# Two PSUM tiles of one bank in place of one tile of two banks, under a transformer block's dense products

## The chip, the cores and the metric

The kernel runs on one core of a Trainium2 chip. The metric is the device time of one execution in microseconds, as a median over runs. The engines are named as in the profile: PE is TensorE's matmuls and PEld its weight loads, DVE is VectorE, ACT is ScalarE, POOL is GpSimd, SP is SyncE, which issues most DMAs here.

## The reference

```python
xn = _layernorm(x)                      # x: 2048 x 512
qkv = xn @ wqkv                         # 32 heads of 16
scores = einsum("bhqd,bhkd->bhqk", q, k) * 16 ** -0.5
o = einsum("bhqk,bhkd->bhqd", softmax(scores), v)
A = o.reshape(B, S, D) @ wo
z = gelu(einsum("bsd,df->bsf", xn, w_in))          # 2048 x 1792
g = einsum("ts,bsf->btf", w_sp, _layernorm(z[..., 896:])) + b_sp
Bm = einsum("bsf,fd->bsd", z[..., :896] * g, w_out)
return x + A + Bm
```

So attention with 32 small heads and a gated MLP with a spatial product run side by side on the same normalised rows, all in float32.

## The kernel before

The kernel keeps attention going as a steady stream on PE and fills the room between with the dense products of everything else. Attention has three operations on PE: maxima (L1259; query by key, whose rowwise maximum DVE takes in L840), scores (L1245; key by query, whose exponential ACT takes in the helper of L86), and values (L1352; four column tiles of 32, eight key tiles in one stretch of 32 matmuls). These three rotate through three PSUM tiles `sl`, each of two banks.

The dense products use a fourth PSUM tile, `dps`, of two banks as well. A dense product runs as pairs of matmuls on 64 rows each: the upper half of the array writes bank 0 while the lower half writes bank 1, then a second pass swaps the halves (`both`, `dense`, L1310). When such a unit is complete, its generator yields the readers:

- `qk_out`, `v_out`, `z2_out` and `z1_out` (12, 5, 16 and 14 units on `dps`): ACT copies bank 0 out, DVE copies bank 1 out.
- `sp_out` and `sp_lone` (the spatial product): DVE multiplies both banks, in two operations.
- `out_` in `mlp_out` (8 units) and `out_` in `attn_out` (8 units): DVE adds the whole tile of 1024 columns to a tile in SBUF, in one operation.

The order of the instructions on each engine is fixed while the program is built, by a planner written in Python. It keeps a clock for each engine (`T`), gives each step a cost (`yield "D", td(512)` is 0.68 us of DVE), takes, when an engine comes free, the task of lowest priority number that is ready, and holds dense matmuls back until `dfree`, the time when it thinks that the readers are done (`rel`). Work that yields twice gives way to whatever was ready in between:

```python
ends[0] = T[k[0]] = s0 + k[1]
queue_up(k[5], k[3], k[4], ends[0] + 0.08)
```

The semaphores are not written by hand: the framework derives them from which tile an instruction reads or writes. On the chip each engine then runs its instructions strictly in the planned order.

Before the planner's stage there is an opening (class `First`, `STEPS`), whose order is written out by hand. It takes its accumulators in turn from `(dps, *sl)`: every fourth one is `dps`. Among these are 4 of the 16 first maxima (L1137 on `dps`). The opening's `n` normalises the two halves of one `xs` tile on two engines, one half on POOL (L1055) and one on ACT (L86). While dense products have no data, a `filler` (L1324) multiplies zeros into the same two banks, to keep PE running.

Of the kernel before, what the change touches and what calls it, by code (L numbers as in the profile page):

```python
# [8 lines left out]
F32 = mybir.dt.float32  # L9
F32R = mybir.dt.float32r  # L10
AF = mybir.ActivationFunctionType
ALU = mybir.AluOpType
AX = mybir.AxisListType
# [3 lines left out]
P = 128  # L17
S = 2048
D = 512
H = 32  # L20
DH = 16
# [47 lines left out]
def fused_block(ctx, tc, x, wqkv, wo, w_in, w_spT, b_sp, w_out, out):  # L69
    nc = tc.nc  # L70
# [5 lines left out]
    ps = ctx.enter_context(tc.tile_pool(name="ps", bufs=1, space=PSUM))  # L76
# [8 lines left out]
    def act(out, in_, func, **kw):  # L85
        return nc.scalar.activation(out, in_, func, **kw)  # L86

    def ta(n):
        return 0.2 + n / 1220.0

    def td(n):
        return 0.15 + n / 960.0
# [6 lines left out]
    zeror = cp.tile([P, P], F32R, name="zeror")  # L99
# [3 lines left out]
    brow = cp.tile([P, 512], F32R, name="brow")  # L103
# [26 lines left out]
    cscr = dr.tile([1, S], F32, name="cscr")  # L130
    bscr = [dr.tile([P, D], F32, name=f"bscr{t}") for t in range(NT)]

    dps = ps.tile([P, 2, 512], F32, tag="d", name="dps", bufs=1)
    sl = [ps.tile([P, 2, 512], F32, tag=f"s{i}", name=f"sl{i}", bufs=1) for i in range(3)]

    steady = []
# [4 lines left out]
    def move(dst, src):  # L141
        nc.sync.dma_start(raw(dst), raw(src))  # L142
# [36 lines left out]
    def lease(tag, n):  # L179
        room[tag] += n  # L180
# [11 lines left out]
    def spawn(gen, prio=2, ready=None):  # L192
        count[0] += 1
        ends[0] = clock() if ready is None else ready
        queue_up(gen, prio, count[0], ends[0])
# [40 lines left out]
    def t512(nm):  # L236
        return big.tile([P, 512], F32, tag="t512", name=nm, bufs=4)
# [125 lines left out]
    def rel():  # L363
        held[0] -= 1
        if not held[0]:
            dfree[0] = ends[0] + 0.1
# [12 lines left out]
    def qk_out(m, g, a):  # L379
        raw_ = t512(f"qr{m}_{a}_{g}")  # L380
        if a == 0:
            yield "A", ta(512)
            act(raw_, dps[:, 0, :], AF.Copy)
        else:
            yield "D", td(512)
            nc.vector.tensor_copy(raw_, dps[:, 1, :])
        rel()
        spawn(qk_split(m, g, a, raw_), 2, ends[0] + 0.08)

# [30 lines left out]
    vdone = {}  # L420

    def v_out(t, bank, k):
        src = (dps if k is None else sl[k])[:, bank, :].rearrange("p (h d) -> p h d", d=DH)
        if bank:
            yield "D", td(512)
            nc.vector.tensor_copy(vhead[:, t, :, :DH], src)
        else:
            yield "A", ta(512)
            act(vhead[:, t, :, :DH], src, AF.Copy)
        if k is None:  # L430
            rel()
        else:
            free_slot(k)
        vdone[t] = ends[0] + 0.1
# [30 lines left out]
    def z2_out(t, z, j):  # L465
        if j == 0:
            yield "A", ta(448)
            act(z[:, 0:448], dps[:, 0, :448], AF.Copy)
        else:
            yield "D", td(448)  # L470
            nc.vector.tensor_copy(z[:, 448:896], dps[:, 1, :448])
        rel()
        if not held[0]:
            spawn(z2_norm(t, z), 2, ends[0] + 0.08)
# [90 lines left out]
    def z1_out(f, g, bank):  # L565
        if bank == 0:
            yield "C", lambda: room["t5"] > 1
            lease("t5", -2)
            x, u = t512(f"z1x_{g}_{f}"), t512(f"z1u_{g}_{f}")
        else:  # L570
            z = piece(f"z1_{g}_{f}")
            x, u = z.bitcast(F32)[:, 0, :], z.bitcast(F32)[:, 1, :]
        if bank == 0:
            yield "A", ta(512)
            act(x, dps[:, 0, :], AF.Copy)
        else:
            yield "D", td(512)
            nc.vector.tensor_copy(x, dps[:, 1, :])
        rel()
        spawn(z1_gelu(f, g, bank, x, u), 2, ends[0] + 0.08)  # L580

# [136 lines left out]

    def sp_out(g, f, bank, z1):
        yield "D", 0.68  # L720
        nc.vector.scalar_tensor_tensor(z1, dps[:, bank, :], 0.5, z1, ALU.mult, ALU.mult)
        rel()
        spawn(h_split(g, f, z1), 2, ends[0] + 0.08)

    def sp_lone(g, f, z1):
        z1b = t512(f"z1b{g}")
        yield "D", 0.68
        nc.vector.scalar_tensor_tensor(z1b, dps[:, 0, :], 0.5, z1, ALU.mult, ALU.mult)
        yield "D", 0.68
        nc.vector.scalar_tensor_tensor(z1, dps[:, 1, :], 0.5, z1, ALU.mult, ALU.mult)  # L730
        rel()
        yield "G", 1.3
        nc.gpsimd.tensor_add(z1, z1, z1b)
        yield from h_split(g, f, z1)
# [40 lines left out]
    def mlp_out():  # L775
        def load_x(t):
            xt = piece(f"xr{t}").bitcast(F32)
            move(xt, x[t * P:(t + 2) * P, :].rearrange("(a p) d -> p a d", p=P))
            return xt

        def out_(t, xt):
            yield "D", 1.22
            nc.vector.tensor_add(xt, dps, xt)
            rel()
            for a in range(2):
                store(bscr[t + a], xt[:, a, :])
            after(2.5, lease, "big", 1)

        for t in range(0, NT, 2):
            xt = load_x(t)  # L790
            if t == NT - 4:
                selectors()
                prepare(wo_, [(g, f"wo{g}", wo[g * P:(g + 1) * P, :], 512) for g in range(1, 4)], spare=(-9,))
            for q in range(2):
                hp = hps.pop(0)
                if t + 2 * q < NT:
                    mlp_load(t + 2 * q, 1 - q)
                if t == NT - 2 and q:
                    ao_load(0)
                if q:  # L800
                    yield "s",
                for f in range(NF + 1):
                    yield from need(lambda: f in wout)
                    h, c = hp[f // 4], slice((f % 4) * P, (f % 4 + 1) * P)
                    ops = lambda _: (h[:, 0, c], h[:, 1, c], wout[f][:, 0, :], wout[f][:, 1, :])
                    yield from dense(1, ops, ops, (q, 1 - q), not q and f == 0, q == 1 and f == NF)
                lease("big", 2)
                if q:
                    yield "e", [out_(t, xt)]
                yield "q",  # L810
        lease("big", NF + 1)
# [20 lines left out]
    mmax = {}  # L832
# [79 lines left out]
    fin = {}  # L912
# [18 lines left out]
    def attn_out():  # L931
        def out_(t):
            yield "C", lambda: mode == "V" or n_pv == N
            yield "D", 1.22
            nc.vector.tensor_add(fin[t], dps, fin[t])
            rel()
            added[t] = ends[0]

        yield from need(lambda: len(wo_) == 3)
        for t in range(0, NT, 2):  # L940
            op = aos.pop(t)
            if t + 2 < NT:
                ao_load(t + 2)
            yield from need(lambda: t // 4 in lasthl and lasthl[t // 4][1] <= clock())
            hl = lasthl[t // 4][0]
            for q in range(2):
                def ops(g, lower):
                    if g < 3:
                        return op[q][:, 0, g, :], op[q][:, 1, g, :], wo_[g][:, 0, :], wo_[g][:, 1, :]
                    u = t + (1 - q if lower else q)  # L950
                    c = slice((u % 4) * P, (u % 4 + 1) * P)
                    return hl[:, 0, c], hl[:, 1, c], wo_[3][:, 0, :], wo_[3][:, 1, :]
                if q:
                    yield "s",
                yield from dense(3, lambda g: ops(g + 1, False), lambda g: ops(g + 1, True), (q, 1 - q), not q, q == 1)
            lease("big", 3 if t % 4 else 2)
            yield "e", [out_(t)]
            yield "q",
# [55 lines left out]
    def run(gen):  # L1014
        for _ in gen:
            pass

    class First:


        def __init__(self, w0r, w0, wvr, wv, braw):
            self.w0r, self.w0, self.wvr, self.wv, self.braw = w0r, w0, wvr, wv, braw
            self.acc, self.rs, self.mv, self.came, self.split_, self.turn = {}, {}, {}, [], [], 0
# [4 lines left out]

        def take(self, *key):
            self.turn += 1  # L1030
            self.acc[key] = (dps, *sl)[self.turn % 4]
            return self.acc[key]

        def s(self, g, h, other):
# [99 lines left out]
        def x(self, kc, t, other):  # L1134
            if 0 not in mmax:
                mmax[0] = at_.tile([P, 2, 4, 4], F32, tag="mm", name="mm0", bufs=2)
            nc.vector.tensor_reduce(mmax[0][:, :, t, kc], self.acc["m", kc, t], AX.X, ALU.max)  # L1137

    def init_rows(a, put):
        for j in range(2):  # L1140
# [5 lines left out]
    with tc.manual_schedule(engines=engines):  # L1146
# [16 lines left out]
        move(braw, b_sp)  # L1163
        init_rows(0, move)
        for _ in range(WARM):
            nc.tensor.matmul(dps[:, 1, :], zeror, brow, start=True, stop=True)
        first = First(w0r, w0, wvr, wv, braw)
        for word in STEPS.split():
            first.step(word)
# [129 lines left out]
            return True  # L1299

        def bank_of(b):
            return dps[:, b, :] if b < 2 else sl[b // 2 - 1][:, b % 2, :]

        def dense_slot():
            nonlocal pe, lastd, spent
# [90 lines left out]
        while n_pv < N or queue or tasks or late or urgent or turn or slots:  # L1396
            t = T["P"]
# [74 lines left out]
```

## Time and profile before

| | |
|---|---|
| median of 3 runs | 1836.43 us (1835.22 to 1838.37) |
| profiled execution, first to last instruction (its span) | 1830.4 us |
| median of the runs less that span | 6.0 us |
| PE, DVE, ACT, POOL busy | 98%, 79%, 66%, 37% of the span |
| mean granted clock of TensorE | 0.999 of full speed |

Of the profiled execution the profile gives the span alone; the 6.0 us beside it are what the runs have around their instructions, plus what one execution differs from another. Matmuls are pipelined, so a busy PE can still wait: the waits are read from the chain that ended last and from the idle time that the timeline gives before an instruction.

### The profile page before, as it was taken

The page shows a single profiled execution, that of the slowest core. Times are in us where ns is not written, and L with a number is a line of the kernel's source. Part 1 is how long each engine was busy: PE and PEld are TensorE (multiplying, and loading weights), DVE is VectorE, ACT ScalarE, POOL GpSimd, SP SyncE. Part 2 cuts the span into 40 slices and gives each one's busy share as a digit, 9 for nine tenths or more (in the row PEclk, how much of TensorE's full clock was granted, in tenths as well). Part 3 has the DMA queues.
Part 4 walks back from the last instruction along what each step waited for, and adds up shares of the span by engine and source line. Part 5 has one row for each costly group of instructions (what it writes and reads, how often), then busy time and mean ns, then how long its engine had stood idle before and what let it go on. Part 6 is the DMA issues. An engine that isn't in the chain of part 4 may idle for free.

```text
span 1830.4 us, 38100 instructions
## 1 busy us (share of the span) xinstructions
PE 1800.6 (98%) x14742; PEld 1087.6 (59%) x14742; DVE 1443.2 (79%) x1696; ACT 1211.4 (66%) x1329; POOL 684.5 (37%) x786
## 2 busy tenths in 40 slices
PE   9999999999999999999999999999999999999998
PEld 6666566666556565565656655656566665656543
DVE  8857787888888787787877887778778877888882
ACT  4257777888877777666666665666666665666655
POOL 5452241777767776212532244103422140002201
PEclk9999999999999999999999999999999999999999
DMA  7876654433664237647757568655757477466423
GB/s 265 280 240 227 201 190 128 123 114 114 180 190 132 95 105 209 163 137 186 227 144 204 159 188 201 166 143 158 190 146 181 141 210 170 121 156 168 136 88 104
DMA packets 214910, 305.64 MB, mean 167 GB/s; under 512 B 37744, under 2 KB 107952, under 8 KB 214720
## 3 DMA queue, kind: packets, MB, share of 16 engines
q1 hardware_dynamic: 207240, 275.93, 53.3%
q0 software_dynamic: 7488, 27.27, 4.3%
q8 instruction: 116, 1.90, 0.4%
q14 instruction: 66, 0.54, 0.1%
HBM read 193.27 MB, written 109.85 MB: 166 GB/s over the span
## 4 chain that ended last, share of the span: by engine, by line
PE 89%; DVE 5%; DMA 3%; issue 1%; SPq 1%; ACT 1%; POOL 0%; DVEq 0%; ACTq 0%; POOLq 0%
PE dps L1310 35%; PE sl L1352 24%; PE sl L1245 14%; PE sl L1259 12%; DVE mm L840 4%; PE dps L1324 1%; SPq L142 1%; DMA wsp_14r<-in_w_spT 1%; DMA zs<-z2scr 1%; DMA mscr<-ms 0%; PE sl L984 0%; DMA x<-in_x 0%; ACT pf L86 0%; DMA qst<-mscr 0%; DMA qst<-qscr 0%
## 5 line engine op out<-in xcount | busy, mean ns | idle before, releaser
L840 DVE TENSOR_REDUCE mm<-sl 128x2 f32<-128x1024 f32 x1008 | 1208.3, 1222 | 186.0 <-PE sl L1259 177.4
L86 ACT ACTIVATE pf<-sl 128x1024 f32<-128x1024 f32 x1024 | 1043.1, 1026 | 326.7 <-PE sl L1245 288.6
L1352 PE MATMUL sl<-pf,vall 128*32 128x512 f32 x4096 | 467.9, 595 | 0.6 <-DVE on L974 0.6
L1245 PE MATMUL sl<-qst,kst 50*128 50x512 f32 x2048 | 434.6, 417 | 7.7 <-DVE mm L840 2.2
L1259 PE MATMUL sl<-kst,qst 48*128 48x512 f32 x2016 | 414.9, 404 | 3.9 <-DVE mm L840 2.6
L1310 PE MATMUL dps<-wsp,zs 64*128 64x512 f32 x2352 | 381.6, 392 | 0.9 <-DMA zs<-z2scr 0.6
L1245 PEld LDWEIGHTS sl<-qst,kst 50*128 50x128 f32 x2048 | 194.4, 184 | 220.3 <-issue 81.6
L1352 PEld LDWEIGHTS sl<-pf,vall 128*32 128x32 f32 x4096 | 119.2, 109 | 266.5 <-issue 234.9
L1259 PEld LDWEIGHTS sl<-kst,qst 48*128 48x128 f32 x2016 | 191.8, 185 | 104.2 <-ACT pf L86 49.5
L1310 PEld LDWEIGHTS dps<-wsp,zs 64*128 64x128 f32 x2352 | 228.7, 187 | 36.8 <-DMA zs<-z2scr 1.2
L86 ACT ACTIVATE e<-sl 128x512 f32<-128x512 f32 x64 | 38.3, 598 | 189.9 <-PE sl L1352 177.8
L1374 DVE TENSOR_TENSOR e<-sl,e 128x512 f32<-128x512 f32 x64 | 44.2, 691 | 130.2 <-PE sl L1352 80.5
L743 POOL TENSOR_TENSOR hhl<-z1i,hhl 128x512 fp32r<-128x512 f32 x28 | 35.9, 1292 | 280.6 <-ACT hhl L86 280.6
L1310 PE MATMUL dps<-w,xt 64*128 64x448 f32 x768 | 110.5, 368 | 1.7
L1310 PE MATMUL dps<-wout,hp 64*128 64x512 f32 x672 | 110.5, 393 | 0.1
L891 POOL TENSOR_TENSOR ob<-ob 128x512 f32<-128x512 f32 (+1 forms) x16 | 20.6, 1287 | 173.0 <-DMA ob<-rscr 173.0
L1310 PEld LDWEIGHTS dps<-w,xt 64*128 64x128 f32 x768 | 73.7, 186 | 16.1 <-issue 8.4
L1310 PEld LDWEIGHTS dps<-wout,hp 64*128 64x128 f32 x672 | 64.2, 187 | 10.4 <-issue 0.6
L397 POOL TENSOR_TENSOR qkhl<-qr,qkhl 128x512 fp32r<-128x512 f32 x24 | 30.3, 1280 | 97.3 <-ACT qkhl L86 83.0
L887 POOL TENSOR_TENSOR ob<-ob 128x512 f32<-128x512 f32 (+1 forms) x16 | 20.6, 1287 | 99.3 <-DMA ob<-escr 99.3
L1310 PE MATMUL dps<-wf,zs 64*128 64x512 f32 x336 | 55.5, 392 | 0.1
L1310 PE MATMUL dps<-xnT,wqk 64*128 64x512 f32 x288 | 47.9, 394 | 0.3
(298 smaller groups left out, 1692.4 us busy)
## 6 DMA issues: line engine op xcount, KB each, us to landing
zs<-z2scr SPq DMA_DIRECT2D x192, 256.0 KB
escr<-e SPq DMA_DIRECT2D x60, 256.0 KB
hscr<-hhl POOLq DMA_DIRECT2D x28, 512.0 KB, 5.9
qst<-qscr SPq DMA_DIRECT2D x60, 192.0 KB
kst<-kscr SPq DMA_DIRECT2D x60, 192.0 KB
qscr<-qkhl SPq DMA_DIRECT2D x16, 512.0 KB
kscr<-qkhl SPq DMA_DIRECT2D x16, 512.0 KB
xt<-xscr SPq DMA_DIRECT2D x64, 128.0 KB
```

What stands on the lines that cost most here:

```text
L86: return nc.scalar.activation(out, in_, func, **kw)
L142: nc.sync.dma_start(raw(dst), raw(src))
L397: nc.gpsimd.tensor_sub(hl[:, 1, :], raw_, hl[:, 0, :].bitcast(F32))
L743: nc.gpsimd.tensor_sub(hl[:, 1, :], z1, hl[:, 0, :].bitcast(F32))
L840: nc.vector.tensor_reduce(mmax[g][:, :, t, kc], sl[k], AX.X, ALU.max)
L887: nc.gpsimd.tensor_add(both_[rows, 0, :], both_[rows, 0, :], both_[rows, 1, :])
L891: nc.gpsimd.tensor_mul(both_[rows, 0, :], both_[rows, 0, :], both_[rows, 1, :])
L1245: nc.tensor.matmul(sl[k][:, j, :], kst[p % 2][rows, kt * P:(kt + 1) * P], qst[p % 2][rows, c * 512:(c + 1) * 512], start=True, stop=True)
L1259: nc.tensor.matmul(sl[k][:, j, :], qst[p % 2][rows, tt * P:(tt + 1) * P], kst[p % 2][rows, kc * 512:(kc + 1) * 512], start=True, stop=True)
L1310: nc.tensor.matmul(bank_of(bank)[:, :w], lhs, rhs, start=go, stop=stop)
L1352: nc.tensor.matmul(sl[k][cols:cols + VW, 0, :], vpack(kt + r, 2 * p + j), pf[:, j * 512:(j + 1) * 512], start=n % CYC == 0, stop=n % CYC = ...
L1374: nc.vector.tensor_add(e, sl[k][:, 0, :], e)
```

## The change

The one PSUM tile of two banks becomes two tiles of one bank each, `dps[0]` and `dps[1]`. Every reader and writer of one bank names its own tile. An operation that read both banks can't any more, and is split: the additions of `mlp_out` and `attn_out` (2 x 8) become two additions of 512 columns, each a step of its own for the planner (0.68 us each, where one of 1.22 us stood), and the 4 maxima of the opening that read `dps` become two reductions each. A small class `Banks` lets the opening index the two tiles as one. The banks, the matmuls and their order up to the first of these additions are the same.

```diff
-    dps = ps.tile([P, 2, 512], F32, tag="d", name="dps", bufs=1)
+    dps = [ps.tile([P, 512], F32, tag=f"d{b}", name=f"dps{b}", bufs=1) for b in range(2)]
...
-            act(raw_, dps[:, 0, :], AF.Copy)
+            act(raw_, dps[0], AF.Copy)
...
-            nc.vector.tensor_copy(raw_, dps[:, 1, :])
+            nc.vector.tensor_copy(raw_, dps[1])
...
         def out_(t, xt):
-            yield "D", 1.22
-            nc.vector.tensor_add(xt, dps, xt)
+            for b in range(2):
+                yield "D", td(512)
+                nc.vector.tensor_add(xt[:, b, :], dps[b], xt[:, b, :])
             rel()
...
             yield "C", lambda: mode == "V" or n_pv == N
-            yield "D", 1.22
-            nc.vector.tensor_add(fin[t], dps, fin[t])
+            for b in range(2):
+                yield "D", td(512)
+                nc.vector.tensor_add(fin[t][:, b, :], dps[b], fin[t][:, b, :])
             rel()
...
+    class Banks:
+        def __init__(self, *banks):
+            self.banks = banks
+        def __getitem__(self, key):
+            return self.banks[key[1]][key[0], key[2]]
...
-            self.acc[key] = (dps, *sl)[self.turn % 4]
+            k = self.turn % 4
+            self.acc[key] = sl[k - 1] if k else Banks(*dps)
...
-            nc.vector.tensor_reduce(mmax[0][:, :, t, kc], self.acc["m", kc, t], AX.X, ALU.max)
+            acc = self.acc["m", kc, t]
+            if isinstance(acc, Banks):
+                for j in range(2):
+                    nc.vector.tensor_reduce(mmax[0][:, j, t, kc:kc + 1], acc[:, j, :], AX.X, ALU.max)
+            else:
+                nc.vector.tensor_reduce(mmax[0][:, :, t, kc], acc, AX.X, ALU.max)
```

The other edits (`v_out`, `z2_out`, `z1_out`, `sp_out`, `sp_lone`, the warm-up matmuls, `bank_of`) replace `dps[:, b, ...]` by `dps[b]` in the same way.

## Rows read from the trace of the kernel before

**Rows 1.** The page, busy time of the engines over the span (us, share, instructions).

```profile
PE 1800.6 (98%) x14742; PEld 1087.6 (59%) x14742; DVE 1443.2 (79%) x1696; ACT 1211.4 (66%) x1329; POOL 684.5 (37%) x786
```

**Rows 2.** The page, chain that ended last, share of the span by line.

```profile
PE dps L1310 35%; PE sl L1352 24%; PE sl L1245 14%; PE sl L1259 12%; DVE mm L840 4%; PE dps L1324 1%; SPq L142 1%; DMA wsp_14r<-in_w_spT 1%; DMA zs<-z2scr 1%; DMA mscr<-ms 0%; PE sl L984 0%; DMA x<-in_x 0%; ACT pf L86 0%; DMA qst<-mscr 0%; DMA qst<-qscr 0%
```

**Rows 3.** Tile dps, ScalarE alone: what it idled for (us, times), and who waited for it.

```profile
  DVE z L578: 5.3, 7
  DVE qr L386: 4.4, 6
  DVE z L471: 1.4, 7
...
  DVE vall L426: 9.8, 4
```

**Rows 4.** Timeline around 31 us: start us, us, engine, line, out<-in; idle before it, its releaser.

```profile
30.95 0.82 ACT L86 ACTIVATE x<-x,rs 128x512 f32<-128x512 f32 x1 [0.39 <-DVE rs L1046]
...
31.01 0.77 POOL L1055 TENSOR_SCALAR x<-x,rs 128x512 f32<-128x512 f32 x1 [0.50 <-DVE rs L1046]
```

**Rows 5.** Chain that ended last, in order of time, 66 to 84 us (start us, us, what).

```profile
69.18 0.61 ACT vall L86
69.81 0.69 DVE vall L426
70.50 3.40 DVE mm L840 x3
...
80.07 0.70 DVE vall L426
```

**Rows 6.** Timeline of TensorE, 66 to 84 us.

```profile
70.56 1.64 PE L1310 MATMUL dps<-qst,xnT 64*128 64x512 f32 x12 [0.95 <-DVE vall L426]
...
79.94 0.40 PE L1259 MATMUL sl<-kst,qst 48*128 48x512 f32 x2
80.82 1.42 PE L1310 MATMUL dps<-qst,xnT 64*128 64x512 f32 x10 [0.48 <-DVE vall L426]
```

**Rows 7.** Chain that ended last, 518 to 532 us.

```profile
524.00 0.61 ACT z1x L86
```

**Rows 8.** Timeline, 520 to 532 us.

```profile
522.13 0.94 ACT L86 ACTIVATE z2u<-z2u 128x896 f32<-128x896 f32 x1
...
524.00 0.60 ACT L86 ACTIVATE z1x<-dps 128x512 f32<-128x512 f32 x1 [0.93 <-DVE z L578]
...
525.56 0.19 PEld L1259 LDWEIGHTS sl<-kst,qst 48*128 48x128 f32 x2 [0.39 <-ACT pf L86]
...
526.18 2.36 DVE L840 TENSOR_REDUCE mm<-sl 128x2 f32<-128x1024 f32 x2 [1.08 <-PE sl L1259]
```

**Rows 9.** Timeline, 192 to 202 us, one stretch of the values.

```profile
196.30 3.64 PE L1352 MATMUL sl<-pf,vall 128*32 128x512 f32 x32
...
196.80 0.60 ACT L86 ACTIVATE qr<-dps 128x512 f32<-128x512 f32 x1 [0.76 <-DVE qr L386]
...
200.44 1.94 ACT L86 ACTIVATE pf<-sl 128x1024 f32<-128x1024 f32 x2 [1.09 <-PE sl L1245]
```

**Rows 10.** Timeline, 771 to 776 us: two half-width reads of dps in a row.

```profile
771.25 1.29 DVE L721 SCALAR_TENSOR_TENSOR z1i<-dps,z1i 128x512 f32<-128x512 f32 x2 [0.39 <-PE dps L1310]
```

**Rows 11.** Timeline, 903 to 910 us: two half-width reads of dps with a maximum between.

```profile
904.31 0.69 DVE L728 SCALAR_TENSOR_TENSOR z1b<-dps,z1i 128x512 f32<-128x512 f32 x1 [0.39 <-PE dps L1310]
...
906.05 0.68 DVE L730 SCALAR_TENSOR_TENSOR z1i<-dps,z1i 128x512 f32<-128x512 f32 x1
```

**Rows 12.** Timeline, 1726 to 1731 us: an addition of both banks, the next dense product.

```profile
1726.97 1.20 DVE L935 TENSOR_TENSOR fin<-dps,fin 128x1024 f32<-128x1024 f32 x1
...
1729.59 0.40 PE L1310 MATMUL dps<-wo,op 64*128 64x512 f32 x2
```

**Rows 13.** Chain that ended last, 60 to 84 us.

```profile
61.25 1.24 DVE mm L1137
```

**Rows 14.** Chain that ended last, 1800 to 1831 us.

```profile
1823.64 1.23 DVE fin L935
```

More of the change, by code (lines that the diff above doesn't have):

```diff
@@ L422, in v_out @@
     def v_out(t, bank, k):
-        src = (dps if k is None else sl[k])[:, bank, :].rearrange("p (h d) -> p h d", d=DH)
+        src = dps[bank] if k is None else sl[k][:, bank, :].rearrange("p (h d) -> p h d", d=DH)
         if bank:
@@ L467, in z2_out @@
             yield "A", ta(448)
-            act(z[:, 0:448], dps[:, 0, :448], AF.Copy)
+            act(z[:, 0:448], dps[0][:, :448], AF.Copy)
         else:
             yield "D", td(448)
-            nc.vector.tensor_copy(z[:, 448:896], dps[:, 1, :448])
+            nc.vector.tensor_copy(z[:, 448:896], dps[1][:, :448])
         rel()
@@ L574, in z1_out @@
             yield "A", ta(512)
-            act(x, dps[:, 0, :], AF.Copy)
+            act(x, dps[0], AF.Copy)
         else:
             yield "D", td(512)
-            nc.vector.tensor_copy(x, dps[:, 1, :])
+            nc.vector.tensor_copy(x, dps[1])
         rel()
@@ L720, in sp_out @@
         yield "D", 0.68
-        nc.vector.scalar_tensor_tensor(z1, dps[:, bank, :], 0.5, z1, ALU.mult, ALU.mult)
+        nc.vector.scalar_tensor_tensor(z1, dps[bank], 0.5, z1, ALU.mult, ALU.mult)
         rel()
@@ L727, in sp_lone @@
         yield "D", 0.68
-        nc.vector.scalar_tensor_tensor(z1b, dps[:, 0, :], 0.5, z1, ALU.mult, ALU.mult)
+        nc.vector.scalar_tensor_tensor(z1b, dps[0], 0.5, z1, ALU.mult, ALU.mult)
         yield "D", 0.68
-        nc.vector.scalar_tensor_tensor(z1, dps[:, 1, :], 0.5, z1, ALU.mult, ALU.mult)
+        nc.vector.scalar_tensor_tensor(z1, dps[1], 0.5, z1, ALU.mult, ALU.mult)
         rel()
@@ L1165, in fused_block @@
         for _ in range(WARM):
-            nc.tensor.matmul(dps[:, 1, :], zeror, brow, start=True, stop=True)
+            nc.tensor.matmul(dps[1], zeror, brow, start=True, stop=True)
         first = First(w0r, w0, wvr, wv, braw)
@@ L1301, in bank_of @@
         def bank_of(b):
-            return dps[:, b, :] if b < 2 else sl[b // 2 - 1][:, b % 2, :]
+            return dps[b] if b < 2 else sl[b // 2 - 1][:, b % 2, :]
         def dense_slot():
```

## Prediction

> **What bounds the kernel now.** I read the page's busy times first: PE is busy for 98% of the span, no other engine for more than 79% [rows 1]. A busy PE can still wait, so the next view is the chain of work that ended last: it runs through PE's dense products, values, scores and maxima for 85% of the span, and through DVE's maxima for 4% [rows 2]. So a wait is worth something only where it stands on this chain. Third, the view of the tile `dps`. The reader is to see there who waits for whom: ACT's copies out of `dps` idle until DVE has made its own copy out of `dps`, 20 times, and DVE's copies into `vall` wait 4 times for ACT's [rows 3]. ACT reads bank 0 and DVE bank 1, and `qk_out` writes two different tiles, so the one thing that its two copies share is `dps`: whichever comes second in the planned order waits for the first. Last, I went through the whole chain in order of time and looked for every read of `dps`, and through the timeline of the stretches around them.
>
> **What the change removes.** With two tiles, ACT's copy and DVE's copy of one unit have nothing in common in PSUM, and the second need not wait for the first. The three places where a read of `dps` by the second engine stands on the chain are these.
>
> 1. The opening's first unit of V. ACT's copy takes 0.61 us from 69.18, then DVE's 0.69 us from 69.81, then DVE's maxima follow [rows 5], and PE's next dense product starts at 70.56 after 0.95 us of idling for DVE's copy [rows 6]. Without the order both copies begin at 69.18. DVE is free again 69.81 - 69.18 = 0.63 us earlier, PE can start on bank 0 when ACT is done (69.79) and on bank 1 right behind (69.87). Both branches gain: 0.63 us.
> 2. The second unit. DVE's copy ends at 80.77 [rows 5]; PE starts a pair of maxima at 79.94, and its next dense product at 80.82, having idled 0.48 us for that copy [rows 6]. Pairs follow each other every 0.25 us (six last 1.64 us [rows 6], one alone 0.40, so five steps of 0.25), so PE could go on at 79.94 + 0.25 = 80.19. ACT's copy is done at 80.05, DVE's could be done before. Gain: 80.82 - 80.19 = 0.63 us; I take 0.62.
> 3. The first unit of z1. DVE's copy comes first; ACT's stands from 522.13 + 0.94 = 523.07 to 524.00 idle for it, and is on the chain [rows 7, 8]. Behind it in ACT's queue wait three exponentials, and PE's next weights for a maximum wait for the first of these until 525.56, DVE's next maximum until 526.18 [rows 8]. Without the wait ACT is 0.93 us earlier; DVE is busy until about 526.18 - 1.08 = 525.10 in any case, which leaves it 1.08 us to move, so the chain gains up to 0.93 us. The filler behind it still waits for DVE's copy, so I take 0.8 us.
>
> Sum removed: 0.63 + 0.62 + 0.8 = 2.05 us. The bounds: 0 where another wait (a DMA) is right behind, and 0.95 + 0.65 + 0.93 = 2.5 us from the idle times.
>
> The other 21 of the 24 waits I cost at nothing. What hides them is the stretch of values that the planner puts behind almost every unit: 3.64 us of PE in which neither bank of `dps` is touched. At 196.80 ACT starts 0.76 us late, and yet it idles 1.09 us before its next exponentials at 200.44 [rows 9]: an earlier copy lengthens that idling. In the z2 units the waits are 1.4 / 7 = 0.2 us each [rows 3], and where DVE's copy is second it stands behind DVE's own maximum, not behind ACT. If that cover were gone, the price is the rival below.
>
> **What it adds.** 16 additions and 4 reductions are split, 20 more instructions on DVE. The trace has the split form: two half-width reads of `dps` in a row last 1.29 us together [rows 10], one addition over both banks 1.20 to 1.23 [rows 12, 14]. So a split costs about 0.08 us, 1.6 us of DVE in all. On the chain stand only one of the reductions (61.25, before the first unit [rows 13]; PE's bank 0 comes free sooner, bank 1 0.06 us later) and the last addition (1823.64 [rows 14]): 0.06 + 0.08 = 0.14 us. The others lie beside a stretch of values. Bounds for these 18: 0, and 18 x 0.08 = 1.4 us if none were covered.
>
> [...]
>
> **What moves.** Until the first of the 16 additions nothing moves in the planned order. From there on, a split addition yields in between, and a task that is ready slips in. `sp_lone` has that form today: its two reads start 1.74 us apart with a maximum between [rows 11], where a pair in a row starts 1.29 - 0.68 = 0.61 apart [rows 10, 11], so the second bank comes free 1.13 us later. The queue behind on DVE is a maximum, which loses nothing (it is the one that went ahead); waiting for the bank is PE's next dense product. The smallest room that I found between the end of such an addition and the next dense product (the last one, at the end, aside) is 1729.59 - 1728.17 = 1.42 us [rows 12], more than 1.13 + 0.08 = 1.21. So I take 0. The stores of a result row block and its later reload are 0.1 to 1.2 us later and needed many us after.
>
> Net: 2.05 - 0.14 = 1.9 us less. On the profiled execution 1830.4 becomes 1828.5; on the median of the runs 1836.43, which is 6.0 us above that span, it becomes **1834.5 us**, 0.10% less. About 0.2%, 3.7 us, is what a measurement of this kernel can tell from no change.
>
> **Rivals.**
>
> *The waits are worth what they show.* All 24 count: ACT's 5.3 + 4.4 + 1.4 = 11.1 us, and 4 x 0.65 us for DVE's (their 9.8 us are mostly waiting for PE) [rows 3, 5], together 13.7 us: 1822.7 us. For it: in the z2 and z1 stretches ACT is loaded, and an exponential that comes earlier frees a PSUM tile earlier. Against it: rows 9 and the chain, on which only three stand. [...] Here the planner still holds both banks until both readers are through.
>
> *The second half of an addition comes too late.* Slower. Place: the 16 additions from 1513 us on. If a maximum and the maximum's closing steps slip in, or the planner, which sees its `dfree` up to 1.1 us later, holds dense products back, PE loses what exceeds the room. It decides from 5.6 us lost in all, 0.35 us for each of the 16: then the gain of 1.9 is gone and 3.7 more. With the whole 1.13 + 0.08 us each it is 19 us: 1853. For it: 1.42 us is little room, and a planned order that shifts can shift further. Against it: `sp_lone`'s 1.13 us of delay today.
>
> *The change doesn't do that.* The order could come from the tile that both copies write (`vall` and `z` are shared). Then only `qk_out`, and `z1_out`, whose two copies write different tiles, gain: 0.8 - 0.14 = 0.7 us, 1835.8 us. Against it: two halves of one tile of x are written by ACT and POOL at the same moment, from 30.95 and 31.01 [rows 4], so a shared SBUF tile orders nobody.
>
> **How the numbers follow.** The forecast as worked out has 0.62; its own range is 1833 to 1837 us, from the bounds of gain and splits and the scatter of the runs (3 us from lowest to highest). The waits being worth more, 0.14 (1823 to 1833). No removal, or a DMA that takes the gain back, 0.12 (1836 to 1838). The late second half, 0.12 (1838 to 1853). Faster by over 0.2% (below 1832.8): the second case and a little of the first, 0.17. Slower by over 0.2% (above 1840.1): most of the last, 0.11. Within: 0.72. The range for 8 in 10 leaves out half of the first rival and of the second: 1830.5 to 1840.
>
> **What would show it.** Right, if ACT's and DVE's copies of one unit start together (69.2, 79, 523), if the idle time of ACT for DVE's copies goes from 11 us to near 0, if PE's idling before the first two V units falls from 0.95 and 0.48 to under 0.35 and 0.1, and if 700 to 1500 us shows each stretch of values a constant 1.5 to 2.5 us earlier. Wrong, if that lead melts at a DMA, if the copies still follow each other, or if the pace changes after 1513 us; a lead that grows between 120 and 520 us would say that the hidden waits were not hidden.

## The result, and the profile after

The changed kernel takes 1838.05 us (median of 20 runs, 1835.27 to 1843.29), the kernel before 1834.64 us (20 runs beside them, 1830.06 to 1838.37). The ratio is 1.0022, 95% interval 1.0014 to 1.0030: slower by 0.22%, about 4 us (the interval is 2.6 to 5.5 us), where a gain of 0.10% was forecast. The profiled execution has a span of 1835.0 us (before: 1830.4) at the same granted clock of 0.999.

First the page's busy times after. DVE has 20 instructions more, PE the same number [rows 1]; PE's 4.6 us more are as much as the span grew, so nothing on this page says where to look.

```profile
PE 1805.2 (98%) x14742; PEld 1090.4 (59%) x14742; DVE 1444.6 (79%) x1716; ACT 1211.0 (66%) x1329; POOL 684.2 (37%) x786
```

The copies do what was forecast. The tile `dps` of the kernel after, ScalarE alone: all waits of ACT for DVE's copies (11.1 us in 20 waits [rows 3]) are gone, and what is left is waiting for PE.

```profile
its engine sat idle before it (us, times) until:
  PE dps L1326: 14.7, 4
  PE dps L249: 4.3, 2
  PE dps L1071: 1.4, 2
```

The timelines of ACT, DVE and PE after, at the first two units of V and at the first unit of z1. Both copies of a unit now begin within 0.5 us of each other, in each of the three units; PE idles 0.25 us ahead of its dense product in place of 0.95, and not at all in place of 0.48 [rows 6].

```profile
69.17 0.60 ACT L86 ACTIVATE vall<-dps 128x512 f32<-128x512 f32 x1 [7.81 <-PE dps L1326]
...
78.77 0.59 ACT L86 ACTIVATE vall<-dps 128x512 f32<-128x512 f32 x1
...
521.96 0.60 ACT L86 ACTIVATE z1x<-dps 128x512 f32<-128x512 f32 x1
```

```profile
69.14 0.69 DVE L426 COPY vall<-dps 128x512 f32<-128x512 f32 x1 [1.08 <-PE dps L1326]
...
78.28 0.68 DVE L426 COPY vall<-dps 128x512 f32<-128x512 f32 x1
...
522.24 0.68 DVE L578 COPY z<-dps 128x512 f32<-128x512 f32 x1
```

```profile
69.82 1.73 PE L1326 MATMUL dps<-qst,xnT 64*128 64x512 f32 x12 [0.25 <-ACT vall L86]
...
79.49 1.35 PE L1326 MATMUL dps<-qst,xnT 64*128 64x512 f32 x10
```

To find where time went, I compared the start of each of the stretches of values in the two traces (after less before, us). The order of PE's instructions is the same up to 1511 us, so the stretches answer to each other:

| stretch that begins, before | 87.95 | 443.65 | 458.28 | 512.65 | 527.89 | 731.20 | 744.14 | 851.37 | 865.00 | 1106.96 | 1135.98 | 1511.64 | 1592.38 | 1815.58 |
|---|---|---|---|---|---|---|---|---|---|---|---|---|---|---|
| after less before | -1.43 | -1.34 | -1.01 | -1.04 | -1.91 | -1.79 | -1.05 | -0.91 | -0.55 | -0.62 | -0.04 | 0.00 | +4.56 | +4.56 |

Three things are to be seen. The opening and the first unit of z1 gave 1.43 and 0.87 us, a little more than forecast. In this pair of traces that lead is worn away in small steps (458, 744, 865, 1120 us and others) until nothing is left at 1511 us. And 4.56 us are lost between 1511 and 1592 us, in six stretches, where the first additions stand; none of the later additions costs anything that shows.

Those six stretches in the windows view, engine by engine (share of the DMA engines and GB/s last). First the kernel before, then the kernel after; shown are the first, third and fifth stretch, and the sum over all six. In both kernels the six hold the same work: 288 dense matmuls, 96 of maxima, 96 of scores.

```profile
1511.64:1525.12 13.48, 13.43 (x112) 7.85 (x111) 11.58 (x15) 8.15 (x9) 0.00 (x0) 1.00 0.99 223
...
1539.10:1552.05 12.95, 12.95 (x112) 8.04 (x111) 10.88 (x15) 7.68 (x8) 0.00 (x0) 1.00 0.83 203
...
1565.72:1578.67 12.95, 12.95 (x112) 7.91 (x110) 10.87 (x15) 7.67 (x8) 0.00 (x0) 1.00 0.76 189
...
sum 80.74, PE 80.44 PEld 48.04 DVE 64.38 ACT 50.48 POOL 0.00; mean PE 13.41 PEld 8.01 DVE 10.73 ACT 8.41 POOL 0.00
```

```profile
1511.64:1524.87 13.23, 12.76 (x102) 7.53 (x100) 11.02 (x16) 7.68 (x9) 0.00 (x0) 1.00 1.06 216
...
1539.35:1552.98 13.63, 12.70 (x100) 7.10 (x98) 10.92 (x16) 7.67 (x9) 0.00 (x0) 1.00 0.61 156
...
1567.46:1582.75 15.29, 14.41 (x118) 9.02 (x116) 11.51 (x16) 8.59 (x9) 0.00 (x0) 1.00 0.63 167
...
sum 85.29, PE 82.69 PEld 49.92 DVE 64.17 ACT 50.29 POOL 0.00; mean PE 13.78 PEld 8.32 DVE 10.70 ACT 8.38 POOL 0.00
```

The first stretch after does 10 matmuls less (38 dense ones in place of 48) in nearly the same time; the third does 12 less and is longer. A dense matmul costs 0.117 us in a run of them (six in 0.70 us in the chain), so these two stretches lose 0.9 and 2.1 us, and the fifth, 2.34 us longer with 6 more, 1.6 us: 4.6 in all.

What happens there is read from the timelines of DVE and PE at the first addition. Before, DVE and then PE:

```profile
1513.64 1.21 DVE L783 TENSOR_TENSOR xr<-dps,xr 128x1024 f32<-128x1024 f32 x1
1515.99 1.23 DVE L840 TENSOR_REDUCE mm<-sl 128x2 f32<-128x1024 f32 x1 [1.14 <-PE sl L1259]
```

```profile
1516.34 0.64 PE L1310 MATMUL dps<-wout,hp 64*128 64x512 f32 x4
1516.92 0.50 PE L1259 MATMUL sl<-kst,qst 48*128 48x512 f32 x2
```

After, DVE and then PE:

```profile
1513.63 0.68 DVE L784 TENSOR_TENSOR xr<-dps,xr 128x512 f32<-128x512 f32 x1
1515.99 1.23 DVE L841 TENSOR_REDUCE mm<-sl 128x2 f32<-128x1024 f32 x1 [1.68 <-PE sl L1275]
1517.13 0.68 DVE L784 TENSOR_TENSOR xr<-dps,xr 128x512 f32<-128x512 f32 x1
```

```profile
1516.92 0.50 PE L1275 MATMUL sl<-kst,qst 48*128 48x512 f32 x2 [0.42 <-ACT pf L86]
1517.27 0.50 PE L1261 MATMUL sl<-qst,kst 50*128 50x512 f32 x2
1517.61 0.75 PE L1326 MATMUL dps<-wout,hp 64*128 64x512 f32 x2
```

The maximum that slips in has no data yet. DVE idles 1.68 us for it with the second half queued behind, and the two halves start 3.50 us apart. PE's first dense product, at 1516.34 us before, comes at 1517.61; in its place the planner has put maxima and scores, and PE waits 0.42 us at the maxima for ACT. These maxima start at 1516.92 us in both kernels; before, dense products fill the time ahead of them.

### The profile page after: what moved, and what is told of

It is laid out like the page before. It is cut to its first block, busy times and chain, and to the rows that moved or that the text cites. A ratio compares the mean times of both kernels' runs of the same rounds, so it can differ in the third digit from the quotient of the medians.

```text
span 1835.0 us, 38159 instructions
## 1 busy us (share of the span) xinstructions
PE 1805.2 (98%) x14742; PEld 1090.4 (59%) x14742; DVE 1444.6 (79%) x1716; ACT 1211.0 (66%) x1329; POOL 684.2 (37%) x786
## 4 chain that ended last, share of the span: by engine, by line
PE 88%; DVE 5%; DMA 3%; issue 1%; POOL 1%; ACT 1%; SPq 0%; DVEq 0%; POOLq 0%; ACTq 0%
PE dps L1326 35%; PE sl L1368 24%; PE sl L1261 14%; PE sl L1275 12%; DVE mm L841 4%; DMA zs<-z2scr 1%; PE dps L1340 1%; DMA wsp_14r<-in_w_spT 1%; POOL wsp L288 1%; ACT pf L86 0%; DMA wsp_2r<-in_w_spT 0%; PE sl L986 0%; POOL wsp L286 0%; PE sl L1326 0%; DMA qscr<-qkhl 0%
```

## The experiments

In what follows a two-tile kernel is one with `dps[0]` and `dps[1]`, a one-tile kernel one with the old `dps`; an addition has cover when it stands beside a stretch of values, in which PE doesn't need `dps`. Theory: the planned order of the split additions costs the 4.6 us, through the first one alone. Rivals: two instructions or two tiles cost it by themselves; each addition loses for itself; DVE's wait costs it, not the plan. The times of the six stretches from the one at 1511.64 us on, in each trace (us), with the dense matmuls in the first, second and third:

| kernel | six stretches | sum | dense |
|---|---|---|---|
| before | 13.48 13.98 12.95 13.67 12.95 13.71 | 80.74 | 48, 48, 48 |
| after | 13.23 14.48 13.63 14.48 15.29 14.19 | 85.29 | 38, 54, 36 |
| e1 | 13.49 14.00 13.01 13.62 12.95 13.67 | 80.74 | 48, 48, 48 |
| e2 | 13.22 14.44 13.66 14.48 15.31 14.21 | 85.32 | 38, 54, 36 |
| e3 | 13.47 13.98 12.91 13.68 12.91 13.67 | 80.63 | 48, 48, 48 |
| e4 | 13.22 14.47 14.77 13.96 12.95 13.66 | 83.04 | 38, 54, 52 |
| e5 | 13.69 13.99 12.94 13.65 12.93 13.67 | 80.87 | 48, 48, 48 |
| e6 | 12.72 14.47 14.80 13.96 12.95 13.69 | 82.59 | 36, 54, 54 |

**e1: two tiles, each addition one planned step.** The same edit in `attn_out`.

```diff
+            yield "D", 1.22
             for b in range(2):
-                yield "D", td(512)
                 nc.vector.tensor_add(xt[:, b, :], dps[b], xt[:, b, :])
```

> The changed kernel, with each of the 16 additions planned as one step of 1.22 us again, in which both halves are issued one behind the other. Theory (the planned order of the additions costs the 4.6 us, and the lead of 1.9 us from the first 528 us is used up at the transfers near 731-743 and 1109-1132 us): the stretches of values begin 1.4 to 1.9 us before those of the kernel before until 731, within 0.2 us of them at 1511, and stay there; span 1830.0 to 1831.0, ratio to the kernel before 0.999 to 1.001. Rival 1 (two instructions, or two tiles, cost the time by themselves, whatever the order): the same loss between 1511 and 1597 us as in the changed kernel, span 1834 to 1835.5, ratio 1.002. Rival 2 (the lead is real and only the additions ate it): span 1828.3 to 1829, ratio 0.9985 to 0.9995.

Measured: 1833.85 us, ratio 0.9994 (0.9985 to 1.0002). The loss is gone to the last hundredth in the sum. The lead did not vanish here: the last stretch begins 1.05 us before that of the kernel before. So the first half of the theory holds, and its second half (that the transfers use up the lead) doesn't in this execution. The ratio fits the theory and rival 2 (the lead reaches the end) alike; its interval doesn't tell them apart.

**e2: one tile, each addition two steps.** In the kernel before:

```diff
-            yield "D", 1.22
-            nc.vector.tensor_add(xt, dps, xt)
+            for b in range(2):
+                yield "D", td(512)
+                nc.vector.tensor_add(xt[:, b, :], dps[:, b, :], xt[:, b, :])
```

> The kernel before, with its one tile of two banks, in which only the 16 additions are two steps of 512 columns. Theory (planned order): no lead at all up to 1511 us, then the loss of 4 to 5 us between 1511 and 1597 us as in the changed kernel; span 1834.4 to 1835.5, ratio 1.0018 to 1.003. Rival 1 (it is the two tiles): no loss, span 1830.2 to 1831.5, ratio 0.9995 to 1.0005. If the lead of the changed kernel were still in its end, this one would be 1.5 to 2 us slower than the changed kernel, span 1836.5 to 1837.

Measured: ratio 1.0023 (1.0014 to 1.0032), and 4.58 us more in the six stretches, as in the kernel after. The tiles have no part in the loss. Its span, 1839.9 us, is above what was expected: this execution also lost 2.4 us in the stretch from 1120 us and 1.5 us in the one from 1416.53, and it has no lead.

**e3 and e4: which addition does it.** e3 is the kernel after with the addition of `t == 0` in `mlp_out` alone as one step (the diff); e4 is e1 with that one alone as two:

```diff
+            if t == 0:
+                yield "D", 1.22
             for b in range(2):
-                yield "D", td(512)
+                if not (t == 0):
+                    yield "D", td(512)
                 nc.vector.tensor_add(xt[:, b, :], dps[b], xt[:, b, :])
```

> The changed kernel, in which only the first of the 16 additions is one step again; the other 15 stay two steps. Theory (a cascade: the first split addition stands late in its stretch of values, its second half falls behind maxima, dense work slips by 10 matmuls, and so the next unit ends behind its stretch instead of ahead of it, where each later addition has no cover): the whole loss goes, though only one of the three additions that lost time is changed; 48 dense matmuls in each stretch from 1511 on; span 1830.0 to 1831.3, ratio 0.999 to 1.001. Rival (each split addition loses for itself): only the first one's loss goes, about 0.9 us, span 1833.5 to 1834.5, ratio 1.0015 to 1.0025.

> The changed kernel, in which only the first of the 16 additions is two steps and the other 15 are one. Theory (cascade): the first stretch from 1511.6 loses 0.9 us of PE (38 dense matmuls in place of 48, in nearly the same time); the next unit ends behind its stretch, and its addition, though one step, has no cover: 0.7 to 1.5 us more are lost in the third stretch (1539 to 1553); the planned order has caught up there (52 dense matmuls), so nothing after it; span 1831.8 to 1833, ratio 1.0005 to 1.0015. Rival (each split addition for itself): 0.9 us in all, nothing in the third stretch, span 1831.0 to 1831.5.

Measured: e3 0.9992 (0.9983 to 1.0), no loss in any of the six stretches, though 15 of 16 additions are split. e4 1.0004 (0.9995 to 1.0013): 2.30 us more than e1 in the six stretches, of which 1.76 in the third stretch (14.77 against 13.01 us, with 4 dense matmuls more, 0.47 us), where the addition is one step. Another 0.34 us go in the fourth, where nothing was expected. e4's span of 1830.4 us is lower than expected because this execution came 2.46 us early to 1511 us. The timelines say why the third stretch loses. First DVE's of the kernel before at its second addition, then DVE's of e4:

```profile
1539.70 1.21 DVE L783 TENSOR_TENSOR xr<-dps,xr 128x1024 f32<-128x1024 f32 x1
```

```profile
1541.22 1.23 DVE L844 TENSOR_REDUCE mm<-sl 128x2 f32<-128x1024 f32 x1 [2.28 <-PE sl L1278]
1542.36 1.28 DVE L787 TENSOR_TENSOR xr<-dps,xr 128x512 f32<-128x512 f32 x2
```

The unit lacks the dense matmuls that the first stretch didn't get, so it ends after the stretch of values and not ahead of it. In the kernel before its addition stands at 1539.70 us, 0.6 us into the 3.6 us of values that begin at 1539.11; here the values begin at 1536.87 and are over when it starts at 1542.36. The cover is gone, for an addition that nobody touched. That is the cascade, and "each for itself" falls with both runs.

**e5: the longer cost alone.** e1 with `yield "D", 2 * td(512)`, 1.37 us, in place of 1.22.

> As the kernel with the additions in one step (e1_one_step), but the one step is planned with 1.37 us (twice 0.68) in place of 1.22: the longer cost of the split form without its giving way. Theory (giving way sets it): each stretch from 1511 us on keeps its 48 dense matmuls and its time, no loss there; the gains of the opening and of the first unit of z1 (2.2 to 2.3 us in all, up to 528 us) stay, less what one execution differs from another at the transfers near 731 and 1120 us; ratio 0.9985 to 1.0. Rival 1 (the cost shifts the plan enough): 2 us or more lost between 1511 and 1597 us, ratio 1.0005 to 1.002. Rival 2 (the gains of the opening do not reach the end): no loss and no gain, ratio 0.9998 to 1.0008.

Measured: 0.9997 (0.9989 to 1.0005), 48 dense matmuls in each stretch and 80.87 us: it is the giving way, not the longer cost. Rival 2 stays open as far as the time goes, since the interval reaches 1; in the trace the last stretch begins 1.13 us before that of the kernel before.

**e6: the plan without the wait.** e1, in which the planner alone is told that the first addition ends later:

```diff
             rel()
+            if not t:
+                dfree[0] += 1.36
```

> As the kernel with the additions in one step (e1_one_step), but after the first addition alone the planner's time for the dense products (dfree) is set 1.36 us later; the two halves themselves are done at once, one behind the other. It splits what the splitting of the first addition did (2.3 us lost) into the plan and the wait on the chip. Theory (the plan: PE's queue holds scores and maxima in place of dense matmuls, and PE, which runs in order, stands at them): the same loss, 1.7 to 2.6 us between 1511 and 1566 us, 0.9 of it in the first stretch. Rival (the wait: DVE's second half stands behind a maximum that waits for PE, and PE's dense matmul behind it): the loss goes, at most 0.5 us there.

DVE's timeline of e6: both halves are done in a row, and the maximum comes behind them.

```profile
1513.37 1.28 DVE L784 TENSOR_TENSOR xr<-dps,xr 128x512 f32<-128x512 f32 x2
1515.73 1.23 DVE L843 TENSOR_REDUCE mm<-sl 128x2 f32<-128x1024 f32 x1 [1.08 <-PE sl L1277]
```

Measured: ratio 1.0011 (1.0001 to 1.002), and 1.85 us more in the six stretches, against 2.30 in e4. So the plan alone, with no half of the addition late on DVE, costs most of what the split costs. How the rest divides is not shown exactly: e6's plan is not quite e4's (36, 54 and 54 dense matmuls against 38, 54 and 52), so the other 0.45 us is a rough figure for DVE's wait, and the wait with the old plan was not run. In the first stretch 0.6 us were lost (12 dense matmuls less, 1.4 us of work, in 0.77 us less time), not 0.9.

**e7: how much of the opening reaches the end.** e1 with 36 matmuls of zeros more at the end of the opening.

```diff
+        for _ in range(36):
+            nc.tensor.matmul(dps[1], zeror, brow, start=True, stop=True)
         steady.append(True)
```

> As the kernel with the additions in one step (e1_one_step), with 36 more matmuls of zeros of 512 columns on PE at the end of the opening, 36 x 0.23 = 8.3 us; the planned order is the same. It measures how much of a shift of the opening reaches the end. Theory (all of it: the transfers near 731 and 1120 us add a few tenths to 2.4 us in any execution, whether it is early or late): the first stretch of values 8.0 to 8.6 us later than in that kernel, the last one 7 to 9.5 us later, ratio to the kernel before 1.003 to 1.0045. Rival (transfers that keep their own time take shifts back): the shift shrinks at 731 and at 1109-1132 us, the last stretch less than 6 us later, ratio below 1.0025.

Measured: 1.0039 (1.0027 to 1.0051). The first stretch begins 9.33 us later than in e1 and the last one 11.92 later; both are above what was expected (in two executions of two-tile kernels the first stretch begins up to 1.9 us apart, and the stretch from 1120 us took 18.03 us in place of 16.10). The ratios of e7 and e1 are 0.45% apart, 8.3 us, as much as was put in. The interval of each ratio is 2 us or so to either side, and of a shift of 8.3 us nothing is taken back that shows: the rival falls, and with it my reading that the transfers absorb a lead. What they do is differ from one execution to the next, in either direction. Over the twelve traces of this study the stretch from 731 us takes 12.48 to 14.09 us and the one from 1120 us 15.46 to 19.08, where the windows view gives a DMA share of 0.96 to 1.06 from 1110 to 1130 us, before and after.

**e8, e9, e10: the other small steps.** Up to here the stretches showed +0.3 to +0.4 us at the same five places in every two-tile kernel, and at none of them in the two one-tile kernels. The chain of the kernel after at the first of them: DVE's maximum has all it waited for, and still is 0.23 us of "issue" late; 448.81 less the end of the matmuls that it reads (448.09 + 0.40) is 0.3 us.

```profile
448.09 0.23 PE sl L1275 x2
448.33 0.25 PE sl L1261 x2
448.57 0.23 issue
448.81 1.24 DVE mm L841
```

In DVE's queue this maximum is the 64th of a group of 128 recorded entries. All such places that stand right behind a wait on a semaphore have the same gap: ten in the kernel after, four in the kernel before, 0.40 or 0.41 us each where 0.04 is usual. Splitting the additions, the reductions and the waits moved all later entries on. So I moved them again, with dummy memsets at the very start of the queue (e8: 7 in e1; e9: as e8, with 6 dummy square roots on ACT; e10: 11 in the kernel before):

```diff
+    pad = cp.tile([P, 8], F32, name="pad")
+    for i in range(7):
+        nc.vector.memset(pad[:, i:i + 1], 0.0)
```

> As the kernel with the additions in one step (e1_one_step), with 7 memsets of one column more at the very start of DVE's queue, where DVE waits for x anyway. Nothing else changes. In the traces so far, whenever the 64th entry of each 128 in DVE's queue stands right behind a wait on a semaphore, it starts 0.40 us behind the end of that wait, and elsewhere 0.04. In the two-tile kernels two maxima on the chain are such entries (in the stretches that begin at 443 and 851 us in the kernel before); they lose 0.33 and 0.38 us in every two-tile kernel, and nothing in the one-tile kernels. Theory (the place in the queue): both losses go; against the kernel before, the stretch from 443 lasts within 0.08 us as long, as does the one from 851; ratio 0.998 to 0.9995. Rival (the losses come from the tiles or their waits): both stay, 0.3 to 0.4 us each.

> As e8_dve_queue_7, with 6 square roots of one column more at the start of ACT's queue, to move its entries as well: in the two-tile kernels an exponential behind a semaphore wait near 1786 us (the 64th of 128 again) starts 0.32 us late, and the stretch from 1781 us lasts 0.27 to 0.29 us longer than in the one-tile kernels. Theory (the place in the queue): that loss goes too, the stretch from 1781 lasts as long as in the kernel before within 0.08 us; ratio 0.998 to 0.9993. Rival: it stays.

> The kernel before, with 11 memsets of one column more at the very start of DVE's queue; nothing else changes. That puts the maximum which starts at 449.77 us in the kernel before on the 64th place of 128 in DVE's queue, and the one at 863.29 us not. Theory (the place in the queue): the stretch from 443.65 to 458.28 us, 14.63 us in the kernel before, lasts 14.9 to 15.0 us; the one from 851.37 to 865.00 us stays at 13.63. Rival (tiles or waits): both stay as they are.

Measured, length of the five stretches in us (named by their start in the kernel before):

| kernel | 443.65 | 851.37 | 1106.96 | 1457.39 | 1780.76 |
|---|---|---|---|---|---|
| before | 14.63 | 13.63 | 12.97 | 13.16 | 8.94 |
| e2 (one tile) | 14.63 | 13.67 | 13.00 | 13.16 | 8.91 |
| after | 14.95 | 13.99 | 13.38 | 13.51 | 9.23 |
| e1 | 14.93 | 14.00 | 13.33 | 13.53 | 9.20 |
| e8 | 14.61 | 13.67 | 12.97 | 13.17 | 9.20 |
| e9 | 14.61 | 13.65 | 12.98 | 13.18 | 8.94 |
| e10 (one tile) | 14.94 | 13.64 | 13.00 | 13.19 | 8.92 |

DVE's timeline at that maximum, in the kernels before and after, in e8 and in e10:

```profile
449.77 1.23 DVE L840 TENSOR_REDUCE mm<-sl 128x2 f32<-128x1024 f32 x1 [0.54 <-ACT pf L86]
```

```profile
448.81 1.23 DVE L841 TENSOR_REDUCE mm<-sl 128x2 f32<-128x1024 f32 x1 [0.92 <-PE sl L1261]
```

```profile
448.92 1.23 DVE L844 TENSOR_REDUCE mm<-sl 128x2 f32<-128x1024 f32 x1 [0.55 <-ACT pf L86]
```

```profile
450.17 1.23 DVE L843 TENSOR_REDUCE mm<-sl 128x2 f32<-128x1024 f32 x1 [0.89 <-PE sl L1248]
```

The idle time before it is that of the kernel before in e8 (0.55 and 0.54) and that of the kernel after in e10 (0.89 and 0.92). Seven memsets of one column take four of the five losses away, six square roots on ACT the fifth, and eleven memsets give the kernel before the first one. It is the place in the queue. (e10 has four losses more that were not foreseen: the stretches from 512.65, 690.74, 1026.57 and 1282.67 us last 0.32, 0.36, 0.28 and 0.18 us longer than before, and a 64th place behind a wait, with the same 0.40 us, falls into each: 526.85, 697.60, 1034.42 and 1294.52. e8 and e9 lose 0.32 and 0.35 us in the stretch from 771.54, where DVE idles 1.99 us in e8 in place of 1.64 before its 64th entry; no wait is recorded right before that one.) As times the two versions are no better: e8 0.9998 (0.9989 to 1.0007), e9 0.9999 (0.9987 to 1.001), both above what was expected; in e9's trace the stretch from 1120 us took 19.08 us. A gain of 1.4 to 1.7 us is not resolved by these intervals. e10 ran once, with 1834.37 us.

## Why the prediction was wrong

*What the change removes: right, a little small.* Forecast 0.63 + 0.62 in the opening and 0.8 in z1, 2.05 us in all. Measured 1.43 and 0.87, 2.30 us. The 0.87 is firm: the z1 stretch lasts 14.33 to 14.39 us in all nine traces of kernels with two tiles. The 1.43 is of one pair of traces: in the eight of these nine without e7's added matmuls the first stretch begins 0.68 to 2.61 us before that of the kernel before, and in the other two of one-tile kernels 0.01 us before and 0.44 behind it. The second unit gave 1.33 - 0.74 = 0.59 us (PE's dense products begin at 79.49 and 69.82 us after), the first 0.74, and the z1 stretch lasts 14.37 us in place of 15.24. The prediction's upper bound has 0.65 us for the second unit; the idle time in its row is 0.48 [rows 6]. ACT's other waits for DVE went to nothing as well, and yet the lead stays the same within 0.2 us from 88 to 443 and from 542 to 731 us: costing them at nothing was right.

*What it adds: right for the term it names.* The last addition's two halves run from 1828.20 to 1829.47 us, 1.27 us against 1.23 [rows 14]: 0.04 us where 0.08 was forecast. The reduction's 0.06 does not show: ACT's first copy starts at 69.17 us, and at 69.18 before. Pairs in a row last 1.28 us in e4 and e6, 0.07 more than one of 1.21.

*What moves: this is the step that failed.* "The smallest room that I found ... is 1.42 us, more than 1.21. So I take 0." The room was about right: at the first addition it is 1516.34 - 1514.85 = 1.49 us. The delay wasn't. It was taken from `sp_lone` (1.74 us between the two starts [rows 11]), where DVE goes from the one to the maximum and on to the other without a pause. At the first addition the maximum that slips in waits for PE, the halves start 3.50 us apart, and the second one ends 1517.81 - 1514.85 = 2.96 us later than the whole addition did. The trace of before had this: DVE's next instruction behind the addition idles 1.14 us for PE. In the five later units of `mlp_out` the halves start 1.33 or 1.34 us apart and dense work resumes 1.3 to 1.5 us behind the end of the second, as I had assumed for all. And a wait on the chip was weighed where the plan was what changed: told that `dfree` is later, the planner puts scores and maxima into PE's queue, 10 dense matmuls slip out of the stretch, and every unit behind ends later until the planner has caught up, at 1592 us. The sign that the prediction gave for this, a pace that changes after 1513 us, is what the traces show. The first addition, split, costs 2.30 us by itself (e4) and 4.56 where the next ones, which it pushes off their cover, are split too; by e3, the other 15 lose nothing on their own. One of them gains: the stretch from 1725.68 us lasts 12.88 to 12.90 us in the three kernels with split additions in `attn_out` (after, e2, e3) and 13.05 to 13.10 in the others.

*The rivals.* "The second half of an addition comes too late" is what happened, by the second of its two branches (the planner holds dense products back), with 4.56 us in three units in place of 0.35 in each of 16. Its chance of 0.12 was too low when the delay had been taken from another place and not read at the first addition. "The change doesn't do that" fell with the copies' starts, and "the waits are worth what they show" with the lead that doesn't grow where the hidden waits went.

*What had no term.* The five places in the queues: 0.32 + 0.36 + 0.41 + 0.35 + 0.29 = 1.73 us. With them the sum comes out: -2.30 + 1.73 + 4.56 + 0.04 = +4.0 us, and 0.22% of 1834.64 is 4.0 us. That it fits so well is in part luck: two smaller places of the same kind (0.18 us in the stretch from 771.54, 0.15 in the one from 1362.93) and the 0.22 us gained from 1725.68 are left out and nearly cancel, the 1.43 us are of one pair of traces, and the interval of the ratio is 2.6 to 5.5 us. That 1838.05 us lies only 3.6 us above the forecast of 1834.5 is luck too: the 1836.43 that the forecast starts from, a median of three runs, is 1.8 us above the 1834.64 of the twenty. What counts is the difference, -1.9 us forecast and about +4 measured. That the transfers take a lead back was my first reading of the traces and is wrong by e7.

What stays open: whether the two tiles with one-step additions gain anything. The stretches say a gain of 2.30 - 1.73 = 0.6 us; e1, e3 and e5 measured 0.9992 to 0.9997, each interval reaching 1. No version here is shown to beat the kernel before.

## What to carry to other kernels

Where a planner writes the order, splitting a step changes the plan, and the plan's cost isn't the 0.08 us of the split: before it is costed at nothing, look at the very first place where the order can change, at what is queued next there, and at whether that has its data. If a split is needed for a dependency, keep both halves in one planned step (e1). And compare traces stretch by stretch before believing a sum: here three effects of 1.7 to 4.6 us lay behind a difference of 4.

## What the runs showed of the hardware

The 64th entry of each 128 recorded in DVE's queue, when it stands right behind a wait on a semaphore, starts 0.40 or 0.41 us behind the end of the wait (ten places in the kernel after, four in the kernel before); 0.04 us is usual. On ACT one such place was tested, with 0.32 to 0.34 us. At one of DVE's ten, at 689.24 us after, the instruction before still runs, and DVE idles 0.00 us. On the chain the gap shows: with it the stretch from 443.65 us lasts 14.95 us after and 14.94 in e10, without it 14.63 before and 14.61 in e8. The page of the kernel before lists two queues whose packets it calls instruction (packets, MB, share of 16 engines):

```profile
q8 instruction: 116, 1.90, 0.4%
q14 instruction: 66, 0.54, 0.1%
```

PE and its weight loads have 29658 recorded entries in that trace; DVE, ACT, POOL and SP have 8442. That would be 255.7 entries of the first for each packet of q8 and 127.9 of the others for each of q14, of 8.2 KB: an estimate from these counts, since the profile doesn't say whose entries a packet holds. One packet of q14 follows the maximum that was moved: between 440 and 460 us the kernel after has a single one, within 449.4 to 450.4 us; e10 has one within 450.8 to 451.9; the kernel before has none from 440 to 456 us and e8 none from 445 to 460. That such a packet is what holds the 64th entry up, no run shows. What is shown is that a few dummy instructions at the start of a queue add or remove 0.3 to 0.4 us at places hundreds of microseconds later, so a difference of that size between two kernels need not come from what was edited there.
